# Weight words scaled into a PSUM bank, and a leaky maximum in two parametric relu passes

## Chip, cores and metric

The kernel runs on one core of one Trainium2 chip. The metric is device time in microseconds for one execution; 1259.81 us is the median of three runs of the kernel before (1259.77 to 1260.94).

## What is computed

Four batches of eight heads go through attention that keeps only the 32 largest scores of each row, and the result goes through two feed-forward layers:

```
scores = q @ k^T / 8;  keep scores >= the row's 32nd largest;  attn = softmax @ v      (4 x 8 x 576 x 64)
x1 = relu(x @ w_in)^2 @ w_out                                                          (2304 x 512 x 2048)
h  = x1 @ w_in';  g = maximum(0.01 * h, h);  out = g @ w_out'
```

All weights arrive as float64. The output is float32.

## The kernel before

**Precision.** A matmul operand is cut into a rounded high part and a rest (`xh` and `xl`, `gh` and `gl`, the two halves of `wi` and `wo`), and three products are summed where one would stand. A float64 weight comes as two 32-bit words. `w_convert_steps` (L475 to L500) makes a float32 and then its two parts from them: two ACT passes scale the low word into `b` and the high word into `c`, two DVE passes (L490, L491) put the bits together, ACT copies the high part into `wi` or `wo` (L495), POOL subtracts it from the whole (L498).

**Attention.** It goes by 144 tiles of 128 query rows, in pairs. A tile's scores (L278) come from PE and are copied out by ACT (L279); DVE finds the 32 largest by four `max` and three `match_replace` instructions over 576 columns (L800, L802); ACT and POOL make the masked exponentials (L297 to L311); PE transposes them (L316, L329), ACT and DVE write the two parts of the transposes (L321, L322), and PE multiplies them with the values (L388).

**Feed-forward.** The 2304 tokens are cut into the six blocks of `BLOCKS`. A pass of a block through a layer is 16 steps (`moe`, L527). Each step makes one 128-wide slice of `h` by 12 matmuls (L552), turns it into `gh` and `gl` (L562 to L574), and adds the slice of the step before to up to four `acc` banks by matmuls at L590 or L592. Layer 1's leaky maximum has two forms: for blocks 0 to 4 two relu passes on ACT and a subtraction on POOL (L569 to L571), for block 5 a scaled copy on ACT and a maximum on DVE (L565, L566). The copy into `gh` (L572) and the subtraction into `gl` (L573) follow. Only block 0's 32 steps convert weights (64 tiles, 128 DVE passes); the parts are stored to DRAM and loaded again by the later blocks.

**PSUM.** Eight banks: three under the tag "att" (`bank()`, L102: scores, transposes, value products), and once the feed-forward has begun one for `h` and four for `acc`.

**What sets the order.** The program is written slot by slot, 16 slots per pair of tiles; events hang on slots, and the feed-forward advances by a credit per slot. From this the framework's scheduler makes the order of each engine's queue, by priorities and by when it believes buffers free; each queue is then executed in order. The conversion runs at a raised priority (`CONVP`), and its first DVE pass is held behind the latest top-k instruction (`behind("dve")`).

Of the kernel before, what the change touches and what calls it, by code (L numbers as in the profile page):

```python
# [8 lines left out]
F = mybir.dt.float32  # L9
R = mybir.dt.float32r  # L10
U = mybir.dt.uint32
AF = mybir.ActivationFunctionType
OP = mybir.AluOpType
# [6 lines left out]
H_SCALE = 2.0 ** -112  # L20
# [28 lines left out]
NS = 6  # L49
NE = 4  # L50
WRB = 4
WCB = 5
KRB = 1
VTB = 2

# [7 lines left out]
KLO_D = ((0, 0), (0, 1))  # L63
QLO_D = (0,)

LEAK2 = 5
GLD = 5


# [1 line left out]
def topk_attention_moe_moe2_kernel(  # L71
# [12 lines left out]
    P = 128  # L84
# [8 lines left out]
    PE, ACT, DVE, POOL, SP = nc.tensor, nc.scalar, nc.vector, nc.gpsimd, nc.sync  # L93

    const = ctx.enter_context(tc.tile_pool(name="const", bufs=1))
    pool = ctx.enter_context(tc.tile_pool(name="work", bufs=2))
# [3 lines left out]
    def bank():  # L100
        return psum.tile([P, 512], F, tag="att", name="att", bufs=3)
# [7 lines left out]
    def behind(key):  # L109

        return tc.issue_after(cur[key].ins) if key in cur else ExitStack()
# [15 lines left out]
    for u in units:  # L127
        for hp in range(NHP):
            n = u["n"]
# [3 lines left out]
            for t in range(2 * n // P):  # L133
                lo, hi = t * P, t * P + P
# [41 lines left out]
    late = {}  # L176
# [176 lines left out]
    def block_x(blk):  # L353

        if "x" not in blk:
            i = SETS[blk["idx"]]
            m = max(x["n"] for x in blocks if SETS[x["idx"]] == i)
            if i == 2:
                ts = [pool.tile([P, 2, m], R, tag="wraw", name="x2", bufs=WRB) for _ in range(NK)]
                blk["x"] = [(t[:, 0], t[:, 1]) for t in ts]  # L360
            else:
                xpool = late["mlp"] if i else pool
                ts = [xpool.tile([P, NK, m], R, tag=f"x{c}{i}", name=f"x{c}{i}", bufs=1) for c in "hl"]
                blk["x"] = [(ts[0][:, c], ts[1][:, c]) for c in range(NK)]
        return blk["x"]
# [81 lines left out]
    def w_alloc(i):  # L447
        wi = pool.tile([P, 2, 512], R, tag="wi", name="wi", bufs=3)
        wo = pool.tile([P, 2, 512], R, tag="wo", name="wo", bufs=4)
        wt[i] = (wi, wo)  # L450
        return wi, wo
# [24 lines left out]
    def w_convert_steps(i):  # L476
        if i >= len(steps) or not fresh[i]:
            return
        w2 = w_alloc(i)
        for raw, w in zip(wraw.pop(i), w2):  # L480
            if W64:
                lo, hi = raw[:, :, 0], raw[:, :, 1]
                c = pool.tile([P, 512], F, tag="wc", name="wc", bufs=WCB)
                cu = c.bitcast(U)
                b = pool.tile([P, 512], U, tag="wc", name="wb", bufs=WCB)
                ACT.activation(b, lo, AF.Copy, scale=L_SCALE, bias=L_BIAS)
                ACT.activation(c, hi.bitcast(F), AF.Copy, scale=H_SCALE)
                yield 0
                with behind("dve"):
                    DVE.scalar_tensor_tensor(b, cu, 3, b, op0=OP.logical_shift_left, op1=OP.bitwise_or)  # L490
                DVE.scalar_tensor_tensor(cu, cu, 0x80000000, b, op0=OP.bitwise_and, op1=OP.bitwise_or)  # L491
                yield 0
            else:
                c = raw
            ACT.activation(w[:, 0, :], c, AF.Copy)  # L495
            yield 0
            with behind("pool"):
                POOL.tensor_tensor(w[:, 1, :], c, w.bitcast(F)[:, 0, :], op=OP.subtract)  # L498
            yield 0

    def w_store(i):
        if i >= len(steps) or not fresh[i]:
            return
        wi, wo = wt[i]
        d = wdram[steps[i][1:]]
        SP.dma_start(d[:, 0:2, :], wi.bitcast(F))
        SP.dma_start(d[:, 2:4, :], wo.bitcast(F))
# [22 lines left out]
    def moe(j, layer):  # L530
        blk = blocks[j]
        n = blk["n"]
        x = block_x(blk)
        base = phases.index((j, layer)) * NF
        na = NK if layer == 0 else n // P
        gs = {}
        for f in range(NF + LAG):
            conv = iter(())
            if f < NF:
                si = base + f  # L540
                w_store(si + 1)
                conv = w_convert(si + 2)
                w_load(si + 2)
                wi, wo = wt.pop(si)
                h = late["psum"].tile([P, 512], F, tag="h", name="h", bufs=1)
                cnt = 0
                if f == 0:
                    mm = [(w, c, 0) for w in range(2) for c in range(NK)] + [(0, c, 1) for c in range(NK)]
                else:
                    mm = [(0, c, y) for c in range(NK) for y in range(2)] + [(1, c, 0) for c in range(NK)]  # L550
                for w, c, y in mm:
                    PE.matmul(h[:, 0:n], lhsT=wi[:, w, c * P:(c + 1) * P], rhs=x[c][y][:, 0:n], start=cnt == 0,  # L552
                              stop=cnt == 3 * NK - 1)
                    cnt += 1
                    if cnt % MQ == 0 and cnt < 3 * NK:
                        next(conv, None)
                        yield
                gh = late["mlp"].tile([P, 512], R, tag="gh", name="gh", bufs=2)
                gl = late["mlp"].tile([P, 512], R, tag="gl", name="gl", bufs=2)
                a = late["mlp"].tile([P, 512], F, tag="ga", name="ga", bufs=2)  # L560
                if layer == 0:
                    ACT.activation(a[:, 0:n], h[:, 0:n], AF.Relu)  # L562
                    ACT.activation(a[:, 0:n], a[:, 0:n], AF.Square)
                elif j >= LEAK2:
                    ACT.activation(a[:, 0:n], h[:, 0:n], AF.Copy, scale=0.01)  # L565
                    DVE.tensor_tensor(a[:, 0:n], a[:, 0:n], h[:, 0:n], op=OP.max)  # L566
                else:
                    b = late["mlp"].tile([P, 512], F, tag="gb", name="gb", bufs=1)
                    ACT.activation(a[:, 0:n], h[:, 0:n], AF.Relu)  # L569
                    ACT.activation(b[:, 0:n], h[:, 0:n], AF.Relu, scale=-0.01)  # L570
                    POOL.tensor_tensor(a[:, 0:n], a[:, 0:n], b[:, 0:n], op=OP.subtract)  # L571
                ACT.activation(gh[:, 0:n], a[:, 0:n], AF.Copy)  # L572
                (DVE if j >= GLD else POOL).tensor_tensor(gl[:, 0:n], a[:, 0:n], gh.bitcast(F)[:, 0:n],  # L573
                                                          op=OP.subtract)  # L574
                gs[f] = (gh, gl, wo)
                next(conv, None)
                yield
            if f >= LAG:
                ff = f - LAG
                if ff == 0:  # L580
                    acc = [late["psum"].tile([P, 512], F, tag="acc", name="acc", bufs=4) for _ in range(na)]
                gh, gl, wo = gs.pop(ff)
                mm = [(c, w, gh) for c in range(na) for w in range(2)] + [(c, 0, gl) for c in range(na)]
                if ff == NF - 1:
                    mm.sort(key=lambda m: m[0])
                for i, (c, w, g) in enumerate(mm):
                    cs = slice(c * P, (c + 1) * P)
                    first, last = ff == 0 and g is gh and w == 0, ff == NF - 1 and g is gl
                    if layer == 0:
                        PE.matmul(acc[c][:, 0:n], lhsT=wo[:, w, cs], rhs=g[:, 0:n], start=first, stop=last)  # L590
                    else:
                        PE.matmul(acc[c], lhsT=g[:, cs], rhs=wo[:, w, :], start=first, stop=last)  # L592
                    if i % 3 == 2:
                        next(conv, None)
                        yield
            for _ in conv:
                pass
            if f < NF:
                w_raw(si + 4)
        for c in range(na):  # L600
            if layer == 0:
                xh, xl = x[c]
                ACT.activation(xh[:, 0:n], acc[c][:, 0:n], AF.Copy)
                DVE.tensor_tensor(xl[:, 0:n], acc[c][:, 0:n], xh.bitcast(F)[:, 0:n], op=OP.subtract)  # L604
            else:
                y = pool.tile([P, 512], F, tag="wc", name="y", bufs=WCB)
                ACT.activation(y, acc[c], AF.Copy)
                for p0, n0, r0 in rows(blk["g0"] + c * P, P):
                    ACT.dma_start(out[r0:r0 + n0, :], y[p0:p0 + n0])
# [16 lines left out]
    for uh in uhs:  # L626
        b, hp, i = uh["b"], uh["hp"], uh.get("di")
# [248 lines left out]
```

## Time and profile before

| | |
|---|---|
| median of three runs | 1259.81 us |
| profiled execution | 1260.58 us, its span 1258.8 us |
| busy share of the span | PE 92%, DVE 80%, ACT 74%, POOL 60% |
| chain that ended last | PE 53%, DVE 28%, ACT 4% |
| granted TensorE clock | 0.96 of full speed (mean) |

A span runs from the first to the last instruction. A busy share is a mean over stretches that have different limits, so the stretches have to be looked at one by one. PE's matmuls are pipelined with modelled ends: a PE that is shown busy may still be waiting for data. Lines named L... are those of the kernel before.

### The profile page before, as it was taken

The numbers are of one execution on the slowest core, as the hardware profiler recorded it, in microseconds if no ns is written. First come the engines' busy times: TensorE is split into PE (matmuls) and PEld (weight loads), VectorE is DVE, ScalarE is ACT, GpSimd is POOL, SyncE is SP. The second block draws the span as 40 slices with busy tenths as digits, with TensorE's granted clock in tenths as the row PEclk, the third lists the DMA queues.
The fourth block names the chain that finished last, engine by engine and source line by source line (L and its number), as shares of the span: only waits on it lengthen the run. The fifth ranks groups of instructions, "written<-read, shape, count | busy, mean of one in ns | idle before, by whom it ended". The sixth has DMA issues, their size and how long they took to land.

```text
span 1258.8 us, 20236 instructions
## 1 busy us (share of the span) xinstructions
PE 1153.8 (92%) x6352; PEld 1003.9 (80%) x6352; DVE 1001.0 (80%) x1944; ACT 930.4 (74%) x2031; POOL 761.4 (60%) x856
## 2 busy tenths in 40 slices
PE   4888877999868988998999999999999999999998
PEld 3666755787646776997899989888878889999897
DVE  7999999899999999899999999999999810111022
ACT  6999989899888896887788787877777754433322
POOL 7977697488778998447765576654466732003300
PEclk9889885999989998998999999999999999999999
DMA  9745468578776675898998878876666569878974
GB/s 309 259 166 202 155 230 275 191 268 287 254 253 220 234 241 179 286 341 262 374 367 289 298 260 285 281 237 230 214 206 217 190 235 362 285 251 318 358 258 142
DMA packets 110522, 323.24 MB, mean 257 GB/s; under 512 B 17488, under 2 KB 25680, under 8 KB 110416
## 3 DMA queue, kind: packets, MB, share of 16 engines
q1 hardware_dynamic: 107776, 317.24, 73.2%
q10 hardware_dynamic: 2640, 4.72, 1.0%
q8 instruction: 51, 0.84, 0.3%
q14 instruction: 55, 0.45, 0.1%
HBM read 254.54 MB, written 67.37 MB: 256 GB/s over the span
## 4 chain that ended last, share of the span: by engine, by line
PE 53%; DVE 28%; ACT 4%; issue 2%; DMA 2%; POOL 2%; ACTq 0%; POOLq 0%; DVEq 0%
PE h L552 22%; PE acc L592 12%; PE acc L590 9%; DVE m L800 8%; DVE w L802 7%; DVE wb L490 5%; DVE wc L491 4%; PE att L388 3%; PE att L316 3%; PE att L377 2%; DVE PTs L322 2%; PE sp L278 1%; PE att L329 1%; DMA sd<-stage 1%; DMA wo<-wd 1%
## 5 line engine op out<-in xcount | busy, mean ns | idle before, releaser
L552 PE MATMUL h<-xh,wi 128*128 128x512 f32 (+2 forms) x1280 | 349.4, 346 | 5.3 <-ACT ga L562 3.3
L800 DVE MAX8 m<-w 128x8 f32<-128x576 f32 x432 | 314.8, 748 | 1.8
L552 PEld LDWEIGHTS h<-xh,wi 128*128 128x128 f32 x1280 | 228.5, 192 | 33.3 <-ACT ga L562 3.7
L573 POOL TENSOR_TENSOR gl<-ga,gh 128x512 fp32r<-128x512 f32 (+2 forms) x160 | 168.8, 1055 | 125.7 <-ACT gh L572 67.3
L298 POOL TENSOR_TENSOR e<-s,e 128x576 f32<-128x576 f32 x144 | 210.2, 1480 | 39.9 <-ACT e L297 38.5
L802 DVE MATCH_REPLACE8 w<-m,w 128x576 f32<-128x576 f32 x288 | 213.0, 742 | 0.6
L552 PE MATMUL h<-xl,wi 128*128 128x512 f32 (+2 forms) x640 | 207.7, 343 | 2.1 <-DVE xl L604 1.9
L590 PE MATMUL acc<-gh,wo 128*128 128x512 f32 (+2 forms) x768 | 156.2, 344 | 2.3 <-ACT gh L572 2.1
L571 POOL TENSOR_TENSOR ga<-ga,gb 128x512 f32<-128x512 f32 (+2 forms) x80 | 84.4, 1055 | 116.4 <-ACT gb L570 116.0
L592 PE MATMUL acc<-wo,gh 128*128 128x512 f32 x576 | 152.0, 398 | 2.8 <-ACT gh L572 2.6
L590 PEld LDWEIGHTS acc<-gh,wo 128*128 128x128 f32 x768 | 126.6, 190 | 13.5 <-ACT gh L572 3.4
L552 PEld LDWEIGHTS h<-xl,wi 128*128 128x128 f32 x640 | 121.9, 192 | 15.1 <-DVE xl L604 4.2
L572 ACT ACTIVATE gh<-ga 128x512 fp32r<-128x512 f32 (+2 forms) x192 | 100.3, 522 | 35.7 <-POOL ga L571 24.1
L297 ACT ACTIVATE e<-s,kf 128x576 f32<-128x576 f32 x144 | 107.1, 780 | 20.1 <-POOL kf L290 14.4
L592 PEld LDWEIGHTS acc<-wo,gh 128*128 128x128 f32 x576 | 103.7, 188 | 22.6 <-ACT gh L572 4.8
L302 ACT ACTIVATE e<-e,kf 128x576 f32<-128x576 f32 x144 | 112.2, 780 | 11.6 <-POOL e L298 8.3
L311 ACT ACTIVATE e<-e,rc 128x576 f32<-128x576 f32 x144 | 104.4, 776 | 14.9 <-DVE rc L307 14.8
L562 ACT ACTIVATE ga<-h 128x512 f32<-128x512 f32 (+2 forms) x96 | 46.8, 487 | 85.3 <-PE h L552 81.5
L800 DVE MAX8 m<-s 128x8 f32<-128x576 f32 x144 | 105.2, 747 | 5.8 <-ACT s L279 5.6
L802 DVE MATCH_REPLACE8 w<-m,s 128x576 f32<-128x576 f32 x144 | 106.9, 743 | 0.6
L316 PE MATMUL att<-ident,e 128*128 128x128 f32 x576 | 92.0, 291 | 10.3 <-DVE xf L394 5.8
L278 PE MATMUL sp<-KTa,q 128*128 128x288 f32 x320 | 72.0, 355 | 28.7 <-ACT stage L279 22.3
(89 smaller groups left out, 2225.1 us busy)
## 6 DMA issues: line engine op xcount, KB each, us to landing
wi<-wd SPq DMA_DIRECT2D x160, 512.0 KB, 5.2
wo<-wd SPq DMA_DIRECT2D x160, 512.0 KB, 5.4
wraw<-in_w_dram SPq DMA_DIRECT2D x64, 512.0 KB, 4.8
sd<-stage SPq DMA_DIRECT2D x72, 288.0 KB, 3.1
s<-sd SPq DMA_DIRECT2D x72, 288.0 KB, 5.0
wd<-wi SPq DMA_DIRECT2D x32, 512.0 KB, 3.8
wd<-wo SPq DMA_DIRECT2D x32, 512.0 KB, 3.6
kraw<-in_k_dram SPq DMA_DIRECT2D x16, 576.0 KB, 4.6
```

What stands on the lines that cost most here:

```text
L297: ACT.activation(e, x, AF.Relu, bias=pr["kf"][:, i:i + 1], scale=-FAR)
L298: cur["pool"] = POOL.tensor_tensor(e, x, e, op=OP.subtract)
L302: ACT.activation(e, e, AF.Exp, bias=pr["nb"][:, i:i + 1], scale=0.125, accum_out=pr["sum"][:, i:i + 1])
L311: ACT.activation(e, e, AF.Copy, scale=pr["rc"][:, i:i + 1])
L316: PE.transpose(ps[:, j * P:(j + 1) * P], t["e"][:, j * P:(j + 1) * P], ident)
L552: PE.matmul(h[:, 0:n], lhsT=wi[:, w, c * P:(c + 1) * P], rhs=x[c][y][:, 0:n], start=cnt == 0, stop=cnt == 3 * NK - 1)
L572: ACT.activation(gh[:, 0:n], a[:, 0:n], AF.Copy)
L573: (DVE if j >= GLD else POOL).tensor_tensor(gl[:, 0:n], a[:, 0:n], gh.bitcast(F)[:, 0:n], op=OP.subtract)
L590: PE.matmul(acc[c][:, 0:n], lhsT=wo[:, w, cs], rhs=g[:, 0:n], start=first, stop=last)
L592: PE.matmul(acc[c], lhsT=g[:, cs], rhs=wo[:, w, :], start=first, stop=last)
L800: cur["dve"] = DVE.max(out=m8[:, x, 8 * r:8 * r + 8], in_=t["s"] if r == 0 else t["w"])
L802: cur["dve"] = DVE.match_replace(out=t["w"], in_to_replace=m8[:, x, 8 * r:8 * r + 8], in_values=t["s"] if r == 0 else t["w"], imm_value=NEG)
```

## The change

The high word of each weight is scaled by ACT into a PSUM bank of the tag "att" and not into an SBUF buffer; both DVE passes then read one operand from PSUM and one from SBUF, and write over the SBUF one. The tag "wc" has four buffers and not five, and a conversion takes one of them where it took two. In layer 1, two ACT passes of `Prelu` with slope 0.01 write `gh` and `a` straight from `h`, for all blocks; POOL's subtraction, DVE's maximum and the copy into `gh` go. In layer 0, `gh` is a `Square` of its own, ahead of the one that makes `a`.

```diff
-WCB = 5
+WCB = 4
...
-                c = pool.tile([P, 512], F, tag="wc", name="wc", bufs=WCB)
-                cu = c.bitcast(U)
-                b = pool.tile([P, 512], U, tag="wc", name="wb", bufs=WCB)
+                b = pool.tile([P, 512], U, tag="wc", name="wc", bufs=WCB)
+                v = bank()
                 ACT.activation(b, lo, AF.Copy, scale=L_SCALE, bias=L_BIAS)
-                ACT.activation(c, hi.bitcast(F), AF.Copy, scale=H_SCALE)
+                ACT.activation(v, hi.bitcast(F), AF.Copy, scale=H_SCALE)
                 yield 0
+                vu, c = v.bitcast(U), b.bitcast(F)
                 with behind("dve"):
-                    DVE.scalar_tensor_tensor(b, cu, 3, b, op0=OP.logical_shift_left, op1=OP.bitwise_or)
-                DVE.scalar_tensor_tensor(cu, cu, 0x80000000, b, op0=OP.bitwise_and, op1=OP.bitwise_or)
+                    DVE.scalar_tensor_tensor(b, vu, 3, b, op0=OP.logical_shift_left, op1=OP.bitwise_or)
+                DVE.scalar_tensor_tensor(b, vu, 0x80000000, b, op0=OP.bitwise_and, op1=OP.bitwise_or)
...
                     ACT.activation(a[:, 0:n], h[:, 0:n], AF.Relu)
+                    ACT.activation(gh[:, 0:n], a[:, 0:n], AF.Square)
                     ACT.activation(a[:, 0:n], a[:, 0:n], AF.Square)
-                elif j >= LEAK2:
-                    ACT.activation(a[:, 0:n], h[:, 0:n], AF.Copy, scale=0.01)
-                    DVE.tensor_tensor(a[:, 0:n], a[:, 0:n], h[:, 0:n], op=OP.max)
                 else:
-                    b = late["mlp"].tile([P, 512], F, tag="gb", name="gb", bufs=1)
-                    ACT.activation(a[:, 0:n], h[:, 0:n], AF.Relu)
-                    ACT.activation(b[:, 0:n], h[:, 0:n], AF.Relu, scale=-0.01)
-                    POOL.tensor_tensor(a[:, 0:n], a[:, 0:n], b[:, 0:n], op=OP.subtract)
-                ACT.activation(gh[:, 0:n], a[:, 0:n], AF.Copy)
+                    ACT.activation(gh[:, 0:n], h[:, 0:n], AF.Prelu, alpha=0.01)
+                    ACT.activation(a[:, 0:n], h[:, 0:n], AF.Prelu, alpha=0.01)
```

The scheduler makes another order of it on every engine. The changed kernel's lines are numbered lower by one to six. On DVE, among the first dozen conversions (`m` and `w` are the top-k tiles, `s_105` and `s_107` scores), the queue before reads:

```order
L802 MATCH_REPLACE w<-m_2796,w 128x576
L800 MAX m_2796<-w 128x8
L802 MATCH_REPLACE w<-m_2796,w 128x576
L490 SCALAR_TENSOR_TENSOR wb<-wc,wb 128x512
L800 MAX m_2796<-w 128x8
L491 SCALAR_TENSOR_TENSOR wc<-wc,wb 128x512
L307 RECIPROCAL rc<-sum 128x2
L490 SCALAR_TENSOR_TENSOR wb<-wc,wb 128x512
L491 SCALAR_TENSOR_TENSOR wc<-wc,wb 128x512
L800 MAX m_2796<-s_105 128x8
```

and now (`att` is the PSUM bank):

```order
L794 MAX m_3080<-w 128x8
L489 SCALAR_TENSOR_TENSOR wc<-att,wc 128x512
L490 SCALAR_TENSOR_TENSOR wc<-att,wc 128x512
L489 SCALAR_TENSOR_TENSOR wc<-att,wc 128x512
L490 SCALAR_TENSOR_TENSOR wc<-att,wc 128x512
L794 MAX m_3080<-s_107 128x8
L796 MATCH_REPLACE w<-m_3080,s_107 128x576
L794 MAX m_3080<-w 128x8
L796 MATCH_REPLACE w<-m_3080,w 128x576
L489 SCALAR_TENSOR_TENSOR wc<-att,wc 128x512
L794 MAX m_3080<-w 128x8
L490 SCALAR_TENSOR_TENSOR wc<-att,wc 128x512
```

The passes stand closer together. Of the 1008 top-k instructions of the program, 216 stood ahead of the first pass and 438 ahead of the last; now 246 and 392 do.

On ACT, from the first read of `h` in a step of layer 1 of block 0 to that step's copy into `gh`, the queue before reads:

```order
L569 ACTIVATE ga<-h 128x512
L570 ACTIVATE gb<-h 128x512
L279 ACTIVATE s_106<-att 128x288
L393 ACTIVATE tmp<-att 64x256
L321 ACTIVATE PTs<-att 128x4x128
L487 ACTIVATE wc<-wraw 128x512
L495 ACTIVATE wi<-wc 128x512
L486 ACTIVATE wb<-wraw 128x512
L487 ACTIVATE wc<-wraw 128x512
L572 ACTIVATE gh<-ga 128x512
```

and now, for two such steps:

```order
L565 ACTIVATE gh<-h 128x512
L566 ACTIVATE ga<-h 128x512
L278 ACTIVATE s_106<-att 128x288
L484 ACTIVATE wc<-wraw 128x512
L494 ACTIVATE wi<-wc 128x512
L278 ACTIVATE s_106<-att 128x288
L484 ACTIVATE wc<-wraw 128x512
L320 ACTIVATE PTs<-att 128x4x128
L485 ACTIVATE att<-wraw 128x512
L484 ACTIVATE wc<-wraw 128x512
L565 ACTIVATE gh<-h 128x512
L566 ACTIVATE ga<-h 128x512
```

`gh` comes straight after `h`, with no wait for POOL in between, and the scaled high words go to `att`. Between the first read of `h` by block 0 and the first by block 1, ACT's queue held the masking pass (`e<-s`) of 26 tiles; now it holds that of 20. ACT's queue has a single table load in both programs, at its start.

## Rows read from the trace of the kernel before

**Rows 1.** Busy us of each engine by stretch (count), granted clock, DMA share, GB/s.

```profile
0.00:164.00 164.00, 126.22 (x640) 102.45 (x640) 154.40 (x332) 146.11 (x369) 131.03 (x196) 0.91 0.64 211
164.00:224.00 60.00, 42.92 (x185) 33.32 (x184) 59.27 (x102) 54.29 (x128) 49.62 (x50) 0.72 0.81 273
224.00:504.00 280.00, 243.98 (x1157) 194.58 (x1156) 267.44 (x429) 239.67 (x490) 230.46 (x190) 0.96 0.68 236
504.00:1001.00 497.00, 488.94 (x2854) 437.88 (x2854) 484.23 (x1017) 391.06 (x826) 301.37 (x362) 0.99 0.80 273
1001.00:1259.00 258.00, 251.72 (x1522) 235.69 (x1520) 35.63 (x67) 99.30 (x222) 48.95 (x60) 1.00 0.77 272
```

**Rows 2.** Groups by line and shape, DVE: count | busy us, mean ns | idle before.

```profile
L800 DVE MAX8 m<-w 128x8 f32<-128x576 f32 x432 | 314.8, 748 | 1.8
...
L490 DVE SCALAR_TENSOR_TENSOR wb<-wc,wb 128x512 uint32<-128x512 uint32 x64 | 72.5, 1133 | 6.4 <-ACT wc L487 6.3
...
L491 DVE SCALAR_TENSOR_TENSOR wc<-wc,wb 128x512 uint32<-128x512 uint32 x64 | 70.2, 1098 | 0.5
...
L322 DVE TENSOR_TENSOR PTs<-att,PTs 128x512 fp32r<-128x512 f32 x108 | 72.4, 678 | 3.4 <-ACT PTs L321 2.5
```

**Rows 3.** Line L490 alone: min/median/max ns, first and last start.

```profile
L490 DVE SCALAR_TENSOR_TENSOR wb<-wc,wb x64: 661/1118/1925, 164.2 to 489.4; 128x512 uint32<-128x512 uint32 x64
```

**Rows 4.** DVE timeline, 319 to 329 us: start, us, instruction.

```profile
319.23 1.92 DVE L490 SCALAR_TENSOR_TENSOR wb<-wc,wb 128x512 uint32<-128x512 uint32 x1
...
321.25 1.74 DVE L491 SCALAR_TENSOR_TENSOR wc<-wc,wb 128x512 uint32<-128x512 uint32 x1
...
327.84 0.68 DVE L491 SCALAR_TENSOR_TENSOR wc<-wc,wb 128x512 uint32<-128x512 uint32 x1
```

**Rows 5.** POOL timeline over the same time.

```profile
318.71 1.89 POOL L298 TENSOR_TENSOR e<-s,e 128x576 f32<-128x576 f32 x1
320.75 1.69 POOL L298 TENSOR_TENSOR e<-s,e 128x576 f32<-128x576 f32 x1 [0.15 <-ACT e L297]
322.40 1.73 POOL L498 TENSOR_TENSOR wo<-wc,wo 128x512 fp32r<-128x512 f32 x1
326.82 0.41 POOL L306 TENSOR_SCALAR sum<-sum 128x2 f32<-128x2 f32 x1 [0.19 <-ACT e L302]
330.92 0.56 POOL L290 TENSOR_TENSOR kf<-m,scales 128x4 f32<-128x4 f32 x1 [3.69 <-DVE m L800]
```

**Rows 6.** Line L490 alone by stretch: DVE busy us (count).

```profile
164.00:224.00 60.00, 12.59 (x10) 0.72 0.81 273
224.00:504.00 280.00, 59.87 (x54) 0.96 0.68 236
```

**Rows 7.** Groups by line and shape, ACT.

```profile
L487 ACT ACTIVATE wc<-wraw 128x512 f32<-128x512 f32 x64 | 43.2, 675 | 4.7 <-DVE wc L491 2.8 <-POOL wi L498 1.3 <-POOL wo L498 0.5
...
L572 ACT ACTIVATE gh<-ga 128x512 fp32r<-128x512 f32 x64 | 40.1, 627 | 7.3 <-POOL ga L571 7.0
...
L563 ACT ACTIVATE ga<-ga 128x512 f32<-128x512 f32 x32 | 20.1, 627 | 0.2
...
L562 ACT ACTIVATE ga<-h 128x512 f32<-128x512 f32 x32 | 18.9, 590 | 14.0 <-PE h L552 11.7 <-DMA sd<-stage 2.3
...
L115 ACT ACT_TABLE_LOAD x1 | 1.3, 1283 | 0.7 <-PEq L863 0.7
```

**Rows 8.** Groups by line and shape: the leaky maximum on POOL and on DVE.

```profile
L571 POOL TENSOR_TENSOR ga<-ga,gb 128x512 f32<-128x512 f32 x32 | 44.5, 1392 | 18.8 <-ACT gb L570 18.5
...
L566 DVE TENSOR_TENSOR ga<-ga,h 128x384 f32<-128x384 f32 x16 | 8.9, 555 | 80.2 <-issue 43.8 <-ACT ga L565 36.4
```

**Rows 9.** Of all stretches of 100 us, the one in which ACT is busiest.

```profile
100.00:200.00 100.00, 78.86 (x400) 63.32 (x400) 98.40 (x197) 93.79 (x238) 81.66 (x103) 0.86 0.60 199
```

**Rows 10.** PE's waits: us in total, times, longest us.

```profile
PE att L278 <- DVE PTs L322: 13.1, 7, 5.5
...
PE att L388 <- DVE PTs L339: 5.0, 7, 1.4
```

More of the change, by code (lines that the diff above doesn't have):

```diff
@@ L64 @@
 QLO_D = (0,)
-LEAK2 = 5
 GLD = 5
```

## The prediction

> **What bounds the kernel now.** I read the busy time by stretch first, with the stretches cut where the work changes [rows 1]. Up to 164 us there is attention alone; from 164 to 504 the weights are converted as well (the first bit pass starts at 164.2, the last at 489.4 [rows 3]) and from about 224 block 0 goes through both layers; from 504 to 1001 attention runs beside blocks 1 to 3; after 1001 only matmuls are left. DVE is busy 94% of the first stretch, 98.8% of the second, 95.5% of the third and 97.4% of the fourth, and 14% of the last. So DVE sets the pace for a thousand microseconds and PE for the last 258, where PE is busy 251.7. PE is also at 98.4% in the fourth stretch. In the third, which the change touches most, PE is busy 244.0 of 280 us, ACT 239.7, POOL 230.5: there DVE is ahead of three engines that are not far behind, and this decides how much of a saving on DVE comes out.
>
> Next, the groups of DVE [rows 2]. The two bit passes of the conversion take 1133 and 1098 ns on average over 512 columns, while the subtraction at L322, of the same width but with one operand in PSUM and one in SBUF, takes 678. The bit passes spread from 661 to 1925 ns [rows 3]. The two timelines side by side tell why [rows 4, 5]: from 318.7 to 324.1 POOL reads SBUF without a break, and the passes at 319.23 and 321.25 take 1.92 and 1.74 us; at 327.84 POOL is idle (its instruction of 326.82 is over at 327.23, the next starts at 330.92), and the pass takes 0.68. The pass itself is a 0.67 us instruction; the rest is waiting for POOL.
>
> A rule of the Trainium skill has it otherwise: the Vector Engine (DVE) Microarchitecture Reference, in "Points that are easy to get wrong", says that a scalar-tensor-tensor instruction with two non-bf16 SBUF sources runs at half rate. By it one operand in PSUM would save each pass 512 cycles of 0.96 GHz, 0.53 us, or 68 us over 128 passes (an estimate from that page; where DVE sets the pace it would make about 1190 of the 1202 reckoned below). The row of 0.68 us with two SBUF sources does not agree.
>
> **The change, part by part.**
>
> *Bit passes.* No row has these passes with an operand in PSUM. The ends are 661 ns (the fastest pass before) and 1118 (the median before, no gain); I take L322's 678, the same width with the same two places of operands. A pair of passes then saves 1133 + 1098 - 2 x 678 = 875 ns; 64 pairs save 56.0 us of DVE. Ten pairs lie between 164 and 224, 54 between 224 and 504 [rows 6]: 8.8 and 47.3 us.
>
> *What this is worth by DVE alone.* If DVE keeps its shares, 164 to 224 shrinks to 60 x (59.27 - 8.75) / 59.27 = 51.1 us, and 224 to 504 to 280 x (267.44 - 47.25) / 267.44 = 230.5: 58.4 us less.
>
> *What ACT allows.* ACT loses the copy into `gh` in 16 steps of block 0's layer 1, 16 x 627 ns = 10.0 us [rows 7], so 229.7 us are left between 224 and 504: more than DVE's 220.2. ACT becomes the longest there. If it takes over the share that DVE has now in this stretch, 95.5%, the stretch is 240.5 us (39.5 less), and 164 to 224 becomes 54.29 / 0.955 = 56.8 (3.2 less). That is 42.7 us. With 93.8%, the most that ACT reaches in any 100 us [rows 9], it is 37.2 us; with the 98.8% that DVE reaches, 52.5.
>
> *The scaled write into PSUM.* No row shows ACT writing PSUM. The same pass into SBUF takes 675 ns [rows 7], a pass of this width that reads PSUM 590; 64 times the difference is 5 us. I take 675, no change. The low-word pass is untouched.
>
> *Parametric relu.* No row shows it. The relu that reads the same 512 columns of `h` takes 590, the slowest pass of this width 675 [rows 7]; I take 590, so two `Prelu` replace two relus one for one, and `h` is let go no later. At 675 the 32 passes in the third stretch cost ACT 2.7 us. In block 5 the scaled copy and the copy into `gh` are two passes as well.
>
> *POOL and DVE freed by it.* POOL loses 80 subtractions (1392 ns at 512 columns), 16 of which, 22 us, lie in the third stretch [rows 8]. This is cover that is needed: at 240 us POOL's 230.5 would be a 96% share; without these 22 us, and without waiting in turn for DVE's passes, it stays below 87%. DVE's 16 maxima in the tail are 8.9 us on an engine that is busy 35.6 of 258 there: nothing.
>
> *Layer 0 and buffers.* `Square` in place of `Copy` for `gh` costs the same 627 ns; `gh` comes one pass earlier, which shortens a wait that hardly shows on PE. Four "wc" buffers for conversions that take one each are more than five for conversions that take two.
>
> *The order.* The scheduler moves six tiles' masking passes out of the third stretch (26 to 20), and so the last conversion stands behind 392 top-k instructions, not 438. The top-k instructions of these tiles go with them, so one stretch sheds what the next one carries. I count nothing for it; as a rival it stands below.
>
> Sum, from the profiled execution's 1260.6 us: 1260.6 - 42.7 = **1218 us**. The profiled execution is 0.8 us above the median of the runs, which is within what is rounded here.
>
> **The rivals.** A difference of 0.2%, 2.5 us, is about what a measurement of this kernel tells from none.
>
> *DVE stays the bound* (ACT yields, because the six tiles' passes have left the stretch): the whole 58.4 us come out, 1202. For it speaks that ACT's load falls further by the moved tiles; against it, that without that relief ACT's 229.7 us would have to fit into 230.5, and PE's 244.0 do not.
>
> *The moved tiles have to be paid for.* If ACT holds the third stretch, DVE idles there and does the six tiles later, where it is at 97.4% already: 6 x 7 x 748 ns = 31.4 us [rows 2]. Then even with the full 58.4 before, 27 us remain: 1233. The order speaks for this; against it, that a third stretch with fewer tiles is itself shorter.
>
> *PE holds the stretch.* Its 244.0 us at the 98.4% of the fourth stretch make 247.9, 32.1 less, and 3.2 before: 1225. PE is shown busy also where a matmul waits for data, so this is an upper end for what PE needs.
>
> *Banks run short: slower.* Each conversion now holds one of the three "att" banks from ACT's write to the end of the second pass; with up to two top-k instructions between the passes that is 0.68 + 0.68 + 0.68 and up to 1.5 us, and PE's scores, transposes and value products want the same three, in a queue executed in order. Behind ACT's write, should it wait for a bank, stand the exponentials and score copies that feed DVE. A wait of PE for such a bank now takes 13.1 / 7 = 1.9 us where DVE holds it for a full transposed tile and 5.0 / 7 = 0.7 for a short one [rows 10]. At 64 such waits on the path, 1.3 us each, the gain of 42.7 turns into a loss of 40: 1301. It decides from 0.67 us per tile on. Against it: 64 holds of 2.0 to 3.5 us are at most 27% of three banks over 280 us, and today's waits of PE on these two rows are 18 us in the whole span.
>
> *A table switch.* The page ScalarE: Activation LUTs, under "Table sets: the hidden batching unit", says in the Trainium skill that a function outside the loaded set needs a load on every switch. By the trace a load takes 1283 ns [rows 7]; if `Prelu` and the exponentials needed different ones, 64 steps of blocks 0 to 3 would pay two each, 164 us, and the time would be near 1382. The built program has a single load at ACT's start, as before, which all but excludes this.
>
> **How the numbers follow.** ACT holds the stretch, 1208 to 1223: 0.40. Moved tiles, 1225 to 1245: 0.21. DVE stays the bound, 1200 to 1208: 0.14. PE holds it, near 1225: 0.10. The gain is eaten by waits for banks and stays within 2.5 us: 0.04. Slower by banks: 0.10; by tables: 0.01. Faster is the sum of the first four, 0.85. The range 1200 to 1245 takes these in and leaves out the last three and some of the edges. The likeliest case's own range is 1208 to 1223.
>
> **What would show it.** In the changed profile the bit passes should all take 0.66 to 0.70 us whatever POOL does (their busy sum near 87 us, from 143); if they still spread, the reading of rows 4 and 5 is wrong. The last pass should end near 440 to 450 us. ACT should be the engine above 94% in the stretch of block 0 and DVE below it; if DVE is there above 95%, the second case holds. The fourth stretch should keep DVE near 97% and be longer only by what the moved tiles take. The stretch of matmuls alone at the end should stay near 258 us. The prediction is wrong in kind if ACT's scaled write or PE's "att" matmuls show idle time ended by the second bit pass of more than 40 us in all, or if a `Prelu` takes over 700 ns.

## The result and the profile after

The changed kernel takes 1238.9 us, median of four runs (1234.9 to 1241.4), beside 1259.8 of the kernel before (four runs, 1257.7 to 1260.9): a ratio of 0.983 with a 95% interval of 0.980 to 0.986. It is faster, inside the range of 1200 to 1245, but by 21 us where 43 were forecast.

The busy time by stretch of the kernel after answers to [rows 1]. A row has busy us and count of PE, of its weight loads (PEld), of DVE, ACT and POOL, then the granted clock, DMA share and GB/s. The last three cuts are the events of [rows 1]: block 0's first matmul (now at 209), block 1's (453), the end of the top-k (987). The cut at 160 is only near the one of before, since the first bit pass now starts at 185.2.

```profile
0.00:160.00 160.00, 125.39 (x637) 100.69 (x638) 151.56 (x326) 142.61 (x361) 132.69 (x196) 0.91 0.66 216
160.00:209.00 49.00, 34.88 (x173) 27.97 (x172) 41.84 (x88) 45.57 (x113) 35.30 (x43) 0.86 0.69 235
209.00:453.00 244.00, 226.67 (x1096) 182.84 (x1095) 193.51 (x362) 216.94 (x442) 168.82 (x164) 0.99 0.84 285
453.00:987.00 534.00, 517.32 (x2988) 459.79 (x2986) 524.68 (x1103) 397.87 (x838) 275.60 (x336) 0.99 0.76 262
987.00:1238.00 251.00, 243.73 (x1467) 223.15 (x1466) 27.54 (x53) 86.46 (x201) 29.72 (x39) 1.00 0.78 270
```

Block 0's stretch is 36 us shorter (280 to 244), and DVE (the third pair of numbers) is no longer its pace: busy 193.5 of 244, idle 50.5, where it was idle 12.6 of 280. The fourth stretch has grown from 497 to 534 us, with DVE at 98%. That is where most of the gain went back.

The bit passes did what was expected. The groups of DVE, and line L489 alone (min/median/max), of the kernel after, for [rows 2] and [rows 3]:

```profile
L489 DVE SCALAR_TENSOR_TENSOR wc<-att,wc 128x512 uint32<-128x512 uint32 x64 | 43.6, 683 | 28.9 <-ACT att L485 28.5
L490 DVE SCALAR_TENSOR_TENSOR wc<-att,wc 128x512 uint32<-128x512 uint32 x64 | 43.5, 681 | 0.7
```

```profile
L489 DVE SCALAR_TENSOR_TENSOR wc<-att,wc x64: 660/681/693, 185.2 to 445.8; 128x512 uint32<-128x512 uint32 x64
```

142.7 us of passes have become 87.1, and the spread from 661 to 1925 ns is now 660 to 693. They no longer depend on what POOL does: by the trace 102 of the 128 overlap a two-operand instruction of POOL, and the longest of all takes 693 ns. POOL's timeline and DVE's side by side, of the kernel after, for [rows 4, 5]:

```profile
309.55 2.82 POOL L297 TENSOR_TENSOR e<-s,e 128x576 f32<-128x576 f32 x2 [0.59 <-ACT e L296]
```

```profile
310.72 0.67 DVE L490 SCALAR_TENSOR_TENSOR wc<-att,wc 128x512 uint32<-128x512 uint32 x1
```

The new idle time ahead of L489 is also in the group's row: 28.5 us until ACT has written the PSUM bank. DVE's waits between 209 and 453 us of the kernel after (us in total, times, longest):

```profile
DVE wc L489 <- ACT att L485: 28.5, 20, 3.6
DVE m L794 <- ACT s L278: 12.0, 9, 3.0
```

On ACT, the new operations cost what their nearest rows did, or less [rows 7]. The groups of ACT after:

```profile
L485 ACT ACTIVATE att<-wraw 128x512 f32<-128x512 f32 x64 | 40.8, 641 | 1.2 <-DVE PTs L338 0.7 <-DVE PTs L321 0.5
...
L565 ACT ACTIVATE gh<-h 128x512 fp32r<-128x512 f32 x32 | 18.9, 590 | 21.0 <-PE h L551 20.9
```

The scaled write waits 1.2 us for a free bank in the whole span.

**Where the time went.** The top-k is DVE's work, so DVE's busy and idle time make up the time of its end. Before, DVE was busy 965.3 us and idle 35.4 until that end at 1000.7; after, busy 911.5 and idle 75.4 until 986.9. So 53.8 us of work went, 40.0 us of idle time came (38 of them in block 0's stretch), and 13.8 us remain. The matmuls that are left then take 250.6 us where they took 258.1.

In block 0's stretch DVE's work fell by 73.9 us, more than the 37 that the passes there lost, because the top-k is spread otherwise. Before, 448 of its 1008 instructions were over when block 1 began; now 397 are. At about 0.748 us each, 51 instructions are 38.1 us, and the fourth stretch has grown by 37.8 (from 504.2 to 1000.7 before, 452.6 to 986.9 after).

### The profile page after: what moved, and what is told of

The parts are those of the page before. It is cut to its first block, busy times and chain, and to the rows that moved or that the text cites. A ratio compares the mean times of both kernels' runs of the same rounds, so it can differ in the third digit from the quotient of the medians.

```text
span 1237.5 us, 20100 instructions
## 1 busy us (share of the span) xinstructions
PE 1148.0 (93%) x6352; PEld 994.4 (80%) x6352; DVE 939.1 (76%) x1928; ACT 889.5 (72%) x1951; POOL 642.1 (52%) x776
## 4 chain that ended last, share of the span: by engine, by line
PE 63%; ACT 16%; DMA 8%; DVE 7%; issue 3%; POOL 2%; ACTq 0%; SPq 0%; POOLq 0%; DVEq 0%
PE h L551 25%; PE acc L584 13%; PE acc L586 12%; DMA wraw<-in_w_dram 5%; PE att L315 3%; PE att L387 3%; DVE m L794 3%; PE att L376 3%; DVE w L796 2%; ACT e L301 2%; DMA kraw<-in_k_dram 2%; ACT e L296 2%; PE sp L277 2%; ACT stage L278 2%; ACT s L278 1%
## 5 line engine op out<-in xcount | busy, mean ns | idle before, releaser
L567 POOL TENSOR_TENSOR gl<-ga,gh 128x512 fp32r<-128x512 f32 (+2 forms) x160 | 162.7, 1017 | 274.3 <-ACT ga L566 124.1
L297 POOL TENSOR_TENSOR e<-s,e 128x576 f32<-128x576 f32 x144 | 203.3, 1431 | 44.0 <-ACT e L296 41.8
L586 PE MATMUL acc<-wo,gh 128*128 128x512 f32 x576 | 159.0, 411 | 11.1 <-ACT gh L565 10.0
L565 ACT ACTIVATE gh<-h 128x512 fp32r<-128x512 f32 (+2 forms) x96 | 46.7, 487 | 143.6 <-PE h L551 143.3
L586 PEld LDWEIGHTS acc<-wo,gh 128*128 128x128 f32 x576 | 102.7, 190 | 46.1 <-ACT gh L565 28.4
L567 DVE TENSOR_TENSOR gl<-ga,gh 128x384 fp32r<-128x384 f32 x32 | 17.9, 559 | 158.2 <-ACT ga L566 105.5
L584 PEld LDWEIGHTS acc<-gh,wo 128*128 128x128 f32 x768 | 126.0, 188 | 11.8 <-ACT gh L562 1.0
L310 ACT ACTIVATE e<-e,rc 128x576 f32<-128x576 f32 x144 | 104.5, 780 | 11.6 <-DVE rc L306 11.4
L315 PE MATMUL att<-ident,e 128*128 128x128 f32 x576 | 87.6, 283 | 8.0 <-ACT s L278 2.8
L277 PE MATMUL sp<-KTa,q 128*128 128x288 f32 x320 | 69.1, 352 | 24.3 <-ACT stage L278 19.6
```

The costliest lines, as they stand in the source:

```text
L277: PE.matmul(ps[:, 0:HALF], lhsT=l, rhs=r, start=i == 0, stop=i == len(mm) - 1)
L297: cur["pool"] = POOL.tensor_tensor(e, x, e, op=OP.subtract)
L310: ACT.activation(e, e, AF.Copy, scale=pr["rc"][:, i:i + 1])
L315: PE.transpose(ps[:, j * P:(j + 1) * P], t["e"][:, j * P:(j + 1) * P], ident)
```

## Experiments

All times are medians with the ratio to the kernel before and its 95% interval; ranges in parentheses are of the runs. "e1" and so on are short names. Line numbers are those of the kernel that a row comes from.

### The two parts apart (e1, e2)

e1 is the kernel before with the passes alone:

```diff
-                c = pool.tile([P, 512], F, tag="wc", name="wc", bufs=WCB)
-                cu = c.bitcast(U)
...
+                v = bank()
...
-                ACT.activation(c, hi.bitcast(F), AF.Copy, scale=H_SCALE)
+                ACT.activation(v, hi.bitcast(F), AF.Copy, scale=H_SCALE)
```

(with the two passes as in the change and four "wc" buffers). e2 is the other half alone: `Prelu` twice in layer 1, `Square` twice in layer 0, and the old passes.

> The bit passes alone go to PSUM; the leaky maximum and the copies into gh stay as before. Theory (the waits of the passes for POOL are what was gained, and ACT takes over as the bound of block 0's stretch): the passes take 0.68 us each, DVE's busy sum falls by 56 us, ACT keeps the 10 us of gh copies in that stretch, and the last matmul-only stretch stays at 237 us from block 4 on: 1240 to 1246 us. Rival (most of the gain is the shorter chain through Prelu): 1252 to 1258.

> Prelu and the two Squares alone; the passes stay in SBUF. Theory: DVE stays the bound up to 1000 us; the passes lose some waits for POOL since POOL does 16 subtractions fewer in their stretch (mean 1.05 us in place of 1.12, 8 us in all), and the tail is 6 us longer from block 4 on as in the changed kernel: 1253 to 1262 us. Rival (Prelu carries the gain): 1240 to 1246.

e1: 1223.1 us (1221.0 to 1225.8), 0.971 [0.968, 0.973], so 16 us faster than the whole change. Its passes take 0.68 us, as expected, but the time is 17 us below the expected range. e2: 1267.4, 1.0053 [1.0032, 1.0073], slower than before and some 5 us above what was expected; its passes lost 2.2 us in all and not 8. All of the gain comes from the passes, and the other half takes part of it away; no run takes `Prelu` and the second `Square` apart. The two do not simply add: alone they are worth 38 us of gain and 7 of loss, together 21 of gain. In e1 the top-k stands just as in the change (397 instructions ahead of block 1): the move of the tiles comes with the passes.

### Why the passes were long (e6)

In the kernel before, POOL's subtraction of the high part is replaced by an instruction that only writes:

```diff
-                POOL.tensor_tensor(w[:, 1, :], c, w.bitcast(F)[:, 0, :], op=OP.subtract)
+                POOL.memset(w.bitcast(F)[:, 1, :], 0.0)
```

> The kernel before, with POOL's subtraction that makes the low half of each weight replaced by a POOL memset of that half to zero (so the low halves of the weights are left out). Theory (a pass with two SBUF inputs waits for a POOL instruction that reads SBUF, for its whole length): a pass that runs beside a memset takes 0.66 to 0.70 us, only those beside POOL's other instructions stay long; the mean falls from 1.12 to 0.9 to 1.0 us. Rival 1 (anything on POOL delays it): passes beside a memset are still over 0.8 us. Rival 2 (the form itself runs at half rate): the mean stays at 1.1 us.

One run: 1241.9 us, passes of 910 and 1019 ns on average, from 1133 and 1098, inside the expected 0.9 to 1.0 us when taken together. The timelines of POOL and DVE of e6, from 318 to 324 us:

```profile
318.83 0.53 POOL L498 MEMSET wi<- 128x512 f32 x1 [1.76 <-PE h L552]
319.61 1.29 POOL L573 TENSOR_TENSOR gl<-ga,gh 128x512 fp32r<-128x512 f32 x1 [0.26 <-ACT gh L572]
320.86 3.73 POOL L298 TENSOR_TENSOR e<-s,e 128x576 f32<-128x576 f32 x2
```

```profile
318.75 0.68 DVE L490 SCALAR_TENSOR_TENSOR wb<-wc,wb 128x512 uint32<-128x512 uint32 x1
...
320.02 1.43 DVE L490 SCALAR_TENSOR_TENSOR wb<-wc,wb 128x512 uint32<-128x512 uint32 x1
321.37 1.92 DVE L491 SCALAR_TENSOR_TENSOR wc<-wc,wb 128x512 uint32<-128x512 uint32 x1
```

Beside the memset a pass takes 0.68 us, as beside an idle POOL; beside POOL's subtraction and masking, which read two SBUF operands, 1.4 to 1.9. By the whole trace of e6, the twelve passes that overlap nothing but memsets take 667 to 692 ns, the 25 beside an idle POOL 669 to 694, and the 86 that overlap a two-operand instruction of POOL 1104 on average. Both rivals fail. So the width of the pass is not what is slow, and POOL being busy isn't either: it is POOL reading SBUF while DVE reads two operands from there. The Trainium skill says the same (SBUF — State Buffer, "Who interferes with whom"): a DVE instruction with two SBUF inputs contends with a GpSimd instruction that reads SBUF, not with one that only writes it. Of all first passes (L490) of e6, more than half are now short; line L490 alone, for [rows 3]:

```profile
L490 DVE SCALAR_TENSOR_TENSOR wb<-wc,wb x64: 665/682/1928, 164.0 to 464.5; 128x512 uint32<-128x512 uint32 x64
```

POOL gains from the change too. Its subtraction for `w_out` in the groups of POOL, of the kernel before and of the kernel after (one of before, 1.73 us long, stands in [rows 5]):

```profile
L498 POOL TENSOR_TENSOR wo<-wc,wo 128x512 fp32r<-128x512 f32 x32 | 47.2, 1476 | 6.6 <-ACT wo L495 6.4
```

```profile
L497 POOL TENSOR_TENSOR wo<-wc,wo 128x512 fp32r<-128x512 f32 x32 | 41.4, 1295 | 17.2 <-ACT wo L494 16.0 <-DMA wraw<-in_w_dram 1.2
```

### The lost 12 us: acc matmuls behind their own slice (e3)

The chief new wait of PE's weight loads (PEld), of the kernel after over the whole span (there is a 4.8 us wait of this kind in the kernel before), and below it what of it shows as idle time of PE itself:

```profile
PEld acc L586 <- ACT gh L565: 28.4, 49, 2.3
...
PE acc L586 <- ACT gh L565: 10.0, 14, 2.0
```

Since `gh` now comes one ACT pass after `h`, the scheduler put its acc matmuls straight behind that slice's own `h`. The timeline of the kernel after, from 1181 us (one step of layer 1 with 384 tokens):

```profile
1181.16 0.86 PE L586 MATMUL acc<-wo,gl 128*128 128x512 f32 x3
...
1181.36 0.49 ACT L565 ACTIVATE gh<-h 128x384 fp32r<-128x384 f32 x1 [3.45 <-PE h L551]
...
1181.90 1.22 PEld L586 LDWEIGHTS acc<-wo,gh 128*128 128x128 f32 x6 [0.32 <-ACT gh L565]
1181.90 1.65 PE L586 MATMUL acc<-wo,gh 128*128 128x512 f32 x6
...
1183.39 2.25 PE L551 MATMUL h<-x,wi 128*128 128x384 f32 x12
...
1185.49 0.86 PE L586 MATMUL acc<-wo,gl 128*128 128x512 f32 x3
```

Between `h` and the acc matmuls of its `gh` stand only three matmuls, 0.7 us; ACT's pass ends at 1181.85, and the weight load has waited 0.32 us for it. The step is 4.33 us long. e3 is the changed kernel with layer 1's acc matmuls held behind the next step's `h` (`lasth` is the last of those matmuls):

```diff
-                        PE.matmul(acc[c], lhsT=g[:, cs], rhs=wo[:, w, :], start=first, stop=last)
+                        with tc.issue_after(lasth.ins) if f < NF else ExitStack():
+                            PE.matmul(acc[c], lhsT=g[:, cs], rhs=wo[:, w, :], start=first, stop=last)
```

> The changed kernel with one edge of order more: in layer 1 the acc matmuls of a slice stand behind the h matmuls of the next step, as the program is written. Theory (in the changed kernel the scheduler put them right after their own slice's h, where PE's weight load waits for the first Prelu 0.3 to 0.5 us in every step): no such wait, the stretch from block 4's first matmul is 237 us again, 6 us less in all there and a few less before: 1229 to 1234 us. Rival (the two Prelu passes hold the h bank longer): that stretch stays at 243 us, 1237 to 1241 in all.

1227.2 us (1227.1 to 1227.9), 0.974 [0.971, 0.976]: 11.8 us come back, a little more than expected, and the rival fails. PE's timeline of e3 at the same place:

```profile
1179.65 0.86 PE L587 MATMUL acc<-wo,gl 128*128 128x512 f32 x3
1180.34 2.27 PE L551 MATMUL h<-x,wi 128*128 128x384 f32 x12
1182.45 1.56 PE L587 MATMUL acc<-wo,gh 128*128 128x512 f32 x6
1183.85 0.86 PE L587 MATMUL acc<-wo,gl 128*128 128x512 f32 x3
```

The step is 4.20 us, 0.13 shorter. That cannot be multiplied by the 96 steps of layer 1, most of which run beside the top-k. By the traces, of 11.4 us of span 5.9 come back until the top-k's end, 2.7 from there to block 4's start and 2.8 after it; the stretch from block 4's first matmul is 240.1 us, where 237 had been expected. e1 is 4 us better still; 2.1 of them lie before the top-k's end, and why is open.

### What holds block 0's stretch (e7, e10, e9, e13)

The forecast had ACT hold this stretch. e1's layer 1 part of it, 335 to 446 us, seemed to say so (ACT, the fourth pair, 97%):

```profile
335.20:445.80 110.60, 105.00 (x498) 85.09 (x499) 95.60 (x180) 107.12 (x217) 99.58 (x96) 0.98 0.86 297
```

e7 (on e3) and e9 (on e1) let POOL copy the high part of `w_out`, 32 passes off ACT; e10 (on e3) has five buffers for the raw weights, since ACT's low-word pass waited 16.2 us for them in block 0's stretch of the kernel after (7.3 in e3); e13 is e9 with the parametric relu in block 0 alone, and e3's hold there, which takes one more ACT pass from each step of the stretch above. For e7, e9 and e13:

```diff
-            ACT.activation(w[:, 0, :], c, AF.Copy)
+            split_hi(w[:, 0, :], c, w is w2[0])
```

(`split_hi` with a false last argument is a POOL pass), for e10

```diff
-WRB = 4
+WRB = 5
```

and for e13, against e9 (in these steps the copy into `gh` goes as well)

```diff
+                elif j == 0:
+                    ACT.activation(gh[:, 0:n], h[:, 0:n], AF.Prelu, alpha=0.01)
+                    ACT.activation(a[:, 0:n], h[:, 0:n], AF.Prelu, alpha=0.01)
                 elif j >= LEAK2:
...
+                        with tc.issue_after(lasth.ins) if f < NF and j == 0 else ExitStack():
```

> The changed kernel with the acc matmuls of layer 1 behind the next step's h, and with the high half of w_out's slices copied by POOL and not by ACT. Theory (ACT bounds block 0's stretch, and POOL, busy 169 of 244 us there, has room): ACT loses 32 passes of 0.52 us from start to start, 17 us, and the stretch shrinks by 8 to 14 us: 1214 to 1220 us. Rival (the raw weights' loads hold the stretch, so that a faster ACT only waits longer for them): 1225 to 1229, with ACT's wait for wraw up from 16 to 25 us or more.

> The changed kernel with the acc matmuls of layer 1 behind the next step's h, and five buffers for the raw weights in place of four. Theory (ACT's 16 us of waits for raw loads in block 0's stretch come from the loads being issued when a buffer falls free): the waits fall below 8 us and the time by 3 to 8 us: 1219 to 1224. Rival (the loads are late because the SP queue stands behind the stores of the converted weights, which wait for POOL): the waits stay, 1225 to 1229.

> The bit passes in PSUM alone, and the same move of w_out's high halves from ACT to POOL. Theory: in layer 1 of block 0 POOL is busy 99.6 of 110.6 us already with its half of the leaky maximum, and 16 copies of about 0.6 us more bring it to the length of the stretch; only layer 0's half of the stretch (ACT 116 of 126 us, POOL 85) can shrink: 1215 to 1221 us. Rival (POOL has room there too): 1208 to 1213. Rival (loads hold it): 1221 to 1226.

> The scaled words in PSUM, w_out's high parts copied by POOL, and in layer 1 the parametric relu for block 0 alone, with its acc matmuls put behind the next step's h; blocks 1 to 5 keep the old leaky maximum. Theory (in block 0's stretch ACT at 97% of layer 1's part holds DVE's saving back; an ACT pass less per step there lets it come through): top-k end near 965 us, 1210 to 1216 us in all. Rival (the middle stretch is paced by DVE and takes back what block 0's stretch gives, as in the runs with the fifth raw buffer and with POOL's copy): 1217 to 1221 us, as the same kernel without parametric relu (1219).

e7 1227.7, 0.974 [0.972, 0.977]; e10 1229.1, 0.975 [0.973, 0.978]; e9 1219.0, 0.967 [0.965, 0.969]; e13 1218.0, 0.966 [0.963, 0.968]. In e7 and e10 block 0's stretch did get shorter (244.0 in e3; 239.5 in e7, and 233.5 in e10, where it begins 4.5 us later) and the end did not move, so both theories missed. The times are near the rivals', but their mechanisms missed too: ACT waited 10.3 us for raw weights in e7, not 25, and no such wait is left in e10. The trace shows where it was given back: in e7 PE begins block 3 at 745.6 us and in e3 at 757.7, but block 3's second layer at 870.6 and 874.0. Its queue has attention tiles between, and DVE has done 885 or 886 top-k instructions at that point in both: as many stood ahead of block 1 (400 and 399), and after it DVE is the pace. e9's time hit, but not by its theory: it is 4 us better than e1, by intervals that overlap, while layer 0's part of block 0's stretch is as long as in e1 (125.7 and 125.8 us) and the whole stretch 8 us longer, with 17 more top-k instructions ahead of block 1 (414). e13 came out as its rival. e13's row for the same stretch as e1's:

```profile
335.10:445.70 110.60, 107.40 (x510) 87.25 (x509) 97.92 (x184) 93.58 (x187) 92.14 (x99) 0.98 0.87 303
```

ACT is at 85% instead of 97%, 13.5 us less work, and the stretch is as long to 0.1 us. So ACT is not what holds it, at least not alone. PE is at 97% (which may include waits for data) and the DMA engines at 87%, 303 GB/s, and five raw buffers did shorten block 0's stretch; which of the two holds it is not settled.

### Tiles kept before block 1 (e14, e15, e16, e17)

Here block 1 is taken up 40 slots later, which raises the tiles that stand ahead of it from 52 (54 in e9) to 56 in the built order: on the change (e14), on e3 (e15), on e9 (e16) and on e13 (e17). The part of the edit that takes it up again is left out:

```diff
+        nxt += {0: 40, 1: -40}.get(j, 0)
...
+                if blk["idx"] == 1:
+                    held_back[slot + 40] = blk
+                    continue
```

> The changed kernel with block 1 taken up 40 slots later in the program and block 0's steps spread over those slots too, so that block 1's first matmul stands behind 56 tiles' transposes and not 52. Theory (DVE's idle time in block 0's stretch, 50 us, is what the saving on the bit passes went into, and it is lost because DVE has to do the moved tiles afterwards at 97%): DVE's idle time before the end of top-k falls from 75 to 55 to 65 us and the end comes 8 to 16 us sooner: 1223 to 1231 us. Rival (the stretch is only longer by what is put into it): 1236 to 1242.

> The same with the acc matmuls of layer 1 behind the next step's h. Theory (two separate losses, which add): 1213 to 1220 us. Rival (either mends the same idle time): 1223 to 1229.

> The bit passes in PSUM alone, w_out's high halves on POOL, and block 1 taken up 40 slots later. Theory: DVE's idle time before the end of top-k falls from 61 to about 50 us: 1206 to 1213 us. Rival: 1217 to 1221, as without the delay.

> The same kernel with block 1 taken up 40 slots later, so that four tiles more lie before it. Theory: DVE's idle time before the end of the top-k falls below 55 us and the time is 1206 to 1213 us. Rival (PE's queue is the next bound; what DVE gains before the end of the top-k, the matmuls alone at the end take back): 1216 to 1220 us, as the same spread without parametric relu (1218).

e14 1236.5, 0.981 [0.980, 0.982], the rival, and not to be told from the change by its interval; e15 1222.6, 0.970 [0.968, 0.971], between theory and rival; e16 1218.0, 0.967 [0.966, 0.968], and e17 1218.7, 0.967 [0.964, 0.969], both the rival. The idle time of DVE until the end of the top-k falls, but what follows it grows:

| kernel | DVE busy, idle until the top-k ends | top-k ends | block 4 begins | span ends |
|---|---|---|---|---|
| before | 965.3, 35.4 | 1000.7 | 1022.2 | 1258.8 |
| after | 911.5, 75.4 | 986.9 | 994.6 | 1237.5 |
| e1 passes alone | 910.5, 68.4 | 978.9 | 983.2 | 1221.9 |
| e3 after, acc held back | 908.4, 72.6 | 981.0 | 986.0 | 1226.1 |
| e14 after, spread | 913.0, 67.6 | 980.6 | 992.2 | 1235.2 |
| e15 e3, spread | 909.9, 60.4 | 970.3 | 983.0 | 1222.5 |
| e9 e1, copy on POOL | 911.3, 61.3 | 972.6 | 978.1 | 1217.5 |
| e13 e9, Prelu in block 0 | 911.5, 66.6 | 978.1 | 975.6 | 1216.8 |
| e16 e9, spread | 911.8, 56.9 | 968.7 | 976.8 | 1216.5 |
| e17 e13, spread | 908.7, 60.4 | 969.1 | 977.3 | 1217.1 |

In the last four the top-k ends anywhere from 969 to 978, while PE begins block 4 at 976 to 978 in all of them and ends 239 to 241 us later. That speaks for PE as the next bound, as e17's rival has it, and more room for DVE bought nothing; no run takes matmuls away, so it is argued, not shown. These four agree within their intervals; each beats the kernel before by 3.3 to 3.4% and has a median 1.6 to 1.7% below the change's, with e9 the simplest of them.

## Why the prediction was right or wrong

**The passes: right.** 678 ns each was forecast and 681 to 683 came; 55.6 us of DVE against 56.0. The reading of rows 4 and 5 (a 0.67 us instruction that waits for POOL's reads) is shown by e6; that POOL reads there without a break passes over 0.15 us of idle time before 320.75, which changes nothing. The half-rate rule of the Trainium skill (Vector Engine (DVE) Microarchitecture Reference, "Points that are easy to get wrong") does not hold for this instruction: with two SBUF sources a pass takes 0.68 us in e6 too, when POOL only writes.

**ACT's operations: right.** 590 ns for `Prelu` of 512 columns against 590. The write into PSUM took 641 where 675 was taken, 2 us over 64 writes. It agrees in sign with the Trainium skill (ScalarE: Activation LUTs, "Step-by-step: what each stage is for"), by which ScalarE reaches PSUM faster than SBUF.

**What ACT allows: the length right, the reason not.** The stretch came out at 243.4 us against 240.5. But ACT was to hold it above 94% with 229.7 us of work, and is at 89% with 216.9: the tiles that left took ACT work with them. e13 has 13.5 us less of it than e1 in the layer 1 part, which is no shorter for that. That this length was near is luck as far as ACT goes.

**From 164 us on: better than forecast.** Block 0 begins 15.3 us sooner, not 3.2, partly because only 4 of the 64 pairs of passes now lie ahead of it, where 10 did: the first pass of the pair took 12.59 us there [rows 6] and takes 2.72 now. What made up the rest is open.

**"The order ... I count nothing for it": the step that failed.** One stretch does shed what the next one carries, but the shedding stretch is not DVE's any more, and the carrying one is. 51 top-k instructions, 38.1 us, moved behind block 1's start, and the fourth stretch grew by 37.8. The other runs bear this out. In e1, without `Prelu`, the same 611 instructions are left there and the stretch is 533.1 us long, beside 534.3; in e14 581 are left and it is 513.8 us, in e16 576 and 508.2. Putting them back is not free either: in e14 block 0's stretch is 15.1 us longer for its 30. The rival "the moved tiles have to be paid for" had this mechanism at 31.4 us and a time of 1233; it had the lower chance, though the built order already showed 26 tiles against 20. The measured 1238.9 lies in that rival's 1225 to 1245 and outside the likeliest case's 1208 to 1223; that it came so near 1233 is in part luck, since that sum's terms were off both ways: 15.3 us ahead of block 0 for 8.9, 36.3 in the third stretch for 49.5, 37.8 given back for 31.4, and 7.5 at the end for nothing.

**"`gh` comes one pass earlier, which shortens a wait that hardly shows on PE": the other way round in layer 1.** The sentence was on layer 0, where it held (the weight loads' waits for `gh` fall from 3.4 to 1.0 us); for layer 1 the sum had no such term. There an earlier `gh` made the scheduler place its matmuls earlier, into a wait for ACT: 28.4 us of waits of the weight loads appear, and 10.0 us of idle time of PE itself; undone alone (e3) it is worth 11.8 us. The rows of before could not show it, the built PE queue could. The last stretch, expected near 258 us, came out at 251, because block 4 now begins 8 us after the top-k's end and not 21; from block 4's start to the end it takes 242.9 us where it took 236.6.

**The other rivals.** Banks: refuted, 1.2 us of ACT's waits and 0.8 of PE's where 43 were needed to lose the gain. A table switch: refuted, `Prelu` runs at the relu's cost. DVE as the bound (1202): did not come, DVE is idle a fifth of the stretch. PE as what holds the third stretch (1225): the stretch came out near this rival's 247.9 us, but PE was to be busy 98.4% of it and is at 93%, so it does not hold it alone. That PE is the next bound of the whole kernel, where e9, e13, e16 and e17 stop at 1218 to 1219, is likely and not shown.

Of the forecast's 42.7 us, then, 51.6 came by block 1's start (15.3 and 36.3), 37.8 went back until the top-k's end, and 7.5 came after it: 21.3 us of span.

## What to carry to other kernels

When a change relieves the bounding engine in one stretch, count the work that crosses the stretch's end, in instructions and microseconds, before and after; a shorter stretch that does less of the bounding engine's work has gained only the difference. An operand that comes earlier can make a scheduler put its reader closer to it, so look at the reader's queue, not only at the writer. And when two parts of a change are independent, time them apart: here one part alone was better than both.

## What the runs showed of the hardware

Two instructions that both read two SBUF operands, one on DVE and one on POOL, lengthen each other: a DVE pass of 0.68 us took up to 1.93, and POOL's weight subtraction of 1.30 took 1.44 to 1.48 on average. With one of the passes' operands in PSUM both are at their short times, whatever the other does: at most 0.693 us for a pass, 1.29 to 1.30 on average for the subtraction. How much of it this kernel carried had not been expected: with POOL's weight subtraction alone turned into a write, and all else as before, the time fell from 1260.7 to 1241.9 us (one run; part of that may be the 0.9 us that POOL itself saves on each of 64 tiles, since the write takes 0.53 us).
